# Linformer attention and SwiGLU on one core: E and F loaded as one stacked tile ahead of k, and the first units' turns in another order

## The chip, the core and the metric

The program runs on one core of a Trainium2 chip. A core has a matrix engine (TensorE, PE in the profile; its weight loads are shown as PEld), a vector engine (VectorE, DVE), an activation engine (ScalarE, ACT), a general engine (GpSimd, POOL) and a queue engine (SyncE, SP). Each runs its own list of instructions in order and waits for others on semaphores. Data comes and goes by DMA; a DMA is issued by SP, ACT or POOL, and all issued ones run on the core's 16 DMA engines. In the profile q1 is the DMA queue of SP, q10 that of ACT and q0 that of POOL. Matmul results go to PSUM, which the kernel divides into pools of banks; a bank is free again when its reader has copied it out.

The metric is the device time of one execution in microseconds, as the median of several runs. Beside it there is one profiled execution, from which all durations come.

## The reference

```python
k_proj = np.einsum('ks,bhsd->bhkd', E, k)        # E, F: 64 x 1024; q, k, v: 8 x 8 x 1024 x 64
v_proj = np.einsum('ks,bhsd->bhkd', F, v)
scores = (1 / sqrt(64)) * q @ k_proj^T            # 8 x 8 x 1024 x 64
attn = softmax(scores)
x = (attn @ v_proj), heads side by side           # 8192 x 512
g = x @ w_gate                                    # 512 x 1536
out = (g * sigmoid(g) * (x @ w_val)) @ w_out      # 8192 x 512
```

Every batch has its k and v projected over the sequence by E and F, from 1024 rows to 64; the attention is over these 64 rows. Its result goes through a gated feed-forward block. All inputs and the output are float32; the kernel multiplies in bfloat16.

## The kernel before

The feed-forward work is done in 16 chunks of 512 tokens (two for each batch), and each chunk in 12 tiles of 128 hidden columns: `f_g` makes the gate tile (four matmuls over x, then a tanh on ACT), `f_v` the value tile (four matmuls, then two VectorE operations that give hT), `f_y` the output. A loop over the 192 tiles (lines 629 to 637) runs these on TensorE, and `run_slot` puts the attention work of the next batches between them. That loop is the bulk of the time. The change does not touch it.

Before the loop stands a start written out by hand (lines 480 to 595), which brings the first chunk's x as early as it can. Its order is the order in the code: `manual_schedule` keeps it, for each engine and for each DMA queue. It does this:

- **Loads.** ACT's queue gets k of heads 0 and 1, k of heads 2 and 3 (two float32 pieces, `kraw`, 0.5 MB each) and then F. SP's queue gets E. POOL's queue casts while it loads and gets, in this order, a part of q, k of heads 4 to 7, the other part of q, v in three pieces, and the weights of hidden tiles 0 and 1 and of the next ones. Some of the weight loads stand in POOL's list behind the normalisations `u_N`.
- **Warming.** `warm(n)` runs n matmuls over zeros, whose results nobody reads.
- **Turning E and F.** The projection needs E and F with the sequence on the partitions. `turn(which, at, halves)` transposes 64x128 pieces on TensorE (lines 504 to 509) and copies four of them at a time to `ET` or `FT` on ACT (line 511, which shows as line 138, the helper `copy`). E is turned after eleven warming matmuls. F is turned in two halves, later, between other work.
- **Projecting k.** VectorE casts the four heads of `kraw` to bfloat16; ACT casts half of the last one (lines 531 to 536). `u_KV` multiplies with `ET` (line 150), first heads 0 to 3 and later 4 to 7; `u_KT0` turns the result and four copies put it into the block diagonal `BD`.
- **Units.** The first chunk has four units (u = 0 to 3: head group g = u // 2, token half i = u % 2). For each, `u_T` turns q, `u_S` makes the scores and their exponentials (lines 271 and 275), `u_R` sums them and takes the reciprocal on VectorE (lines 286 and 288), `u_N` multiplies (line 301, on POOL), and `u_A` turns the normalised unit (line 317) and copies it to `AT`.
- **Projecting v, and x.** `u_V0` multiplies v with `FT` (lines 170 to 185), `u_PV2` and `u_PV1` make x from `AT` and the projected v (lines 343 and 355), one or two head pairs and 256 tokens at a time.
- **The first tiles.** `f_mm(c, f, w, i)` (line 377) makes the half i (256 tokens) of hidden tile f; w is 0 for the gate and 1 for the value. Four such groups, for the first 256 tokens of tiles 0 and 1, stand among the last turns of the units (lines 576 to 582).

The PSUM pool "pa" (`ps_a`, letter "a") has three banks, used in turn by `u_T`, `u_A`, `u_PV2` and `u_PV1` and, before, by F's turn. Pools "g" and "v" have two banks each, pool "y" one.

Of the kernel before, what the change touches and what calls it, by code (L numbers as in the profile page):

```python
# [12 lines left out]
BF16 = mybir.dt.bfloat16  # L13
FP32 = mybir.dt.float32
# [3 lines left out]
S = 1024  # L18
D = 64
KP = 64  # L20
DM = H * D
DFF = 1536
P = 128
NJ = S // P
# [10 lines left out]
def kernel(  # L35
# [19 lines left out]
    nc = tc.nc  # L55
    scale = 1.0 / float(D) ** 0.5

    const = ctx.enter_context(tc.tile_pool(name="const", bufs=1))
# [15 lines left out]
    BD = [const.tile([P, H, P], BF16, name=f"BD{i}") for i in range(2)]  # L74
    BDV = [const.tile([P, NPAIR, P], BF16, name=f"BDV{i}") for i in range(2)]
    ks = [const.tile([P, H, D], BF16, name=f"ks{i}") for i in range(2)]
    ET = const.tile([P, NJ, KP], BF16, name="ET")
    FT = const.tile([P, NJ, KP], BF16, name="FT")

    wg = w_pool.tile([P, NKT, DFF], BF16, name="wg")  # L80
    wv = w_pool.tile([P, NKT, DFF], BF16, name="wv")
# [51 lines left out]
    def bank(where, shape, dt, name):  # L133
        pool, tag = banks[where]
        return pool.tile(shape, dt, name=name, tag=tag)

    def copy(eng, out, in_):
        (nc.scalar.copy if eng is nc.scalar else eng.tensor_copy)(out=out, in_=in_)  # L138
# [152 lines left out]
    def u_N(b, u, eng=nc.gpsimd):  # L291
        ch, w = divmod(u, 4)
        g, i = divmod(w, 2)
        if (b, ch) in BY_DMA:
            if (b, ch, "d") not in AA:
                AA[b, ch, "d"] = aw.tile([P, 4, H, KP], BF16, name="AAd", tag="AAd")
            a = AA[b, ch, "d"][:, 2 * i : 2 * i + 2, 4 * g : 4 * g + 4, :]
        else:
            a = AA[b, u] = aw.tile([P, 2, 4, KP], BF16, name="AA", tag="AA", bufs=4)
            a = a[:]  # L300
        eng.tensor_tensor(  # L301
            out=a.rearrange("p j h k -> p h j k"),
            in0=ee.pop((b, u))[:],
            in1=rr.pop((b, u))[:].unsqueeze(3).to_broadcast([P, 4, 2, KP]),
            op=ALU.mult,
        )
# [45 lines left out]
    def u_PV1(b, ch, pr, i, eng):  # L352

        ps = ps_a.tile([P, CW // 2], FP32, name="pv", tag="pa")
        nc.tensor.matmul(
            out=ps[:].rearrange("p (j t) -> p j t", t=P),
            lhsT=BDV[b % 2][:, pr, :],
            rhs=AT[b, ch][:, 2 * i : 2 * i + 2, pr, :],
            start=True,
            stop=True,  # L360
        )
        copy(eng, xT[b, ch][:, pr, 256 * i : 256 * (i + 1)], ps[:])
# [4 lines left out]
    half = {}  # L367
# [109 lines left out]

    with tc.manual_schedule():

        kb[0] = kv_pool.tile([P, H, NJ, D], BF16, name="kb", tag="kb")  # L480
        kraw = [aw.tile([P, 2, NJ * D], FP32, name="kraw", tag=tag) for tag in ("qTd", "AAd")]
        for i in range(2):
            nc.scalar.dma_start(
                out=kraw[i][:],
                in_=k[0, 2 * i : 2 * i + 2].rearrange("h (p j) d -> p h (j d)", j=NJ),
            )
        ef = []
        for which, src in (("E", E), ("F", F)):
            raw = const.tile([KP, S], FP32, name=f"{which}raw")
            (nc.sync if which == "E" else nc.scalar).dma_start(out=raw[:], in_=src)  # L490
            ef.append(raw)
        load_q(0, 0, (0, 2))
        load_k(0, 4, 8)
        zeros = const.tile([P, CW], BF16, name="zeros")
        nc.vector.memset(zeros[:], 0.0)
        make_identity(nc, ident_fp[:])
        make_identity(nc, ident_bf[:])
        nc.vector.memset(ks[0][64:P], 0.0)

        def turn(which, at, halves=(0, 1)):  # L500
            for half in halves:
                ps = bank(at, [P, 4, KP], FP32, "efp")
                for i in range(4):
                    j = 4 * half + i
                    nc.tensor.transpose(
                        out=ps[:, i, :],
                        in_=ef[which][:, bass.ds(j, P, step=NJ)],
                        identity=ident_fp[:KP, :KP],
                    )
                js = slice(4 * half, 4 * half + 4)  # L510
                copy(nc.scalar, (ET, FT)[which][:, js, :], ps[:])

        def warm(n):

            ps = bank("v", [P, CW], FP32, "warm")
            for _ in range(n):
                nc.tensor.matmul(
                    out=ps[:], lhsT=zeros[:, 0:P], rhs=zeros[:],
                    start=True, stop=True,
                )  # L520


        dve, act = nc.vector, nc.scalar
        load_q(0, 0, (2, 4))
        load_v(0, (0, 4, 6, 8))
        load_w_gv(0, 1)
        load_w_gv(1, 2, (0,))
        warm(11)
        turn(0, "v")
        warm(4)  # L530
        for h in range(4):
            for n in range(2):
                eng = act if (h, n) == (3, 1) else dve
                ds = slice(256 * n, 256 * (n + 1)) if h == 3 else slice(0, 512)
                if n == 0 or h == 3:
                    copy(eng, kb[0][:, h].rearrange("p j d -> p (j d)")[:, ds], kraw[h // 2][:, h % 2, ds])
        nc.vector.memset(BD[0][:], 0.0)
        u_KV(0, "k", (0, 4), at="y")
        warm(1)
        u_T(0, 0, "a", act)  # L540
        u_KT0((0, 2), "vg", (dve, dve, dve, act))
        turn(1, "a", (0,))
        u_T(0, 2, "a", act)
        u_S(0, 0, "g")
        u_R(0, 0)
        u_N(0, 0)
        load_w_gv(1, 2, (1,))
        load_w_gv(2, 4, (0,))
        turn(1, "a", (1,))
        warm(1)  # L550
        u_KV(0, "k", (4, 8), at="y")
        warm(1)
        u_KT0((2, 4), "vg", (dve, dve, act, act))
        u_T(0, 1, "a", dve)
        u_T(0, 3, "a", dve)
        u_S(0, 2, "g")
        u_A(0, 0, dve)
        u_R(0, 2)
        u_N(0, 2)
        u_S(0, 1, "g")  # L560
        u_R(0, 1)
        u_N(0, 1)
        u_S(0, 3, "v")
        u_R(0, 3)
        u_N(0, 3)
        u_V0(0, 2, "y")
        u_PV2(0, 0, 0, 0, act)
        warm(1)
        u_V0(2, 3, "y")
        u_A(0, 2, act)  # L570
        u_V0(3, 4, "v")
        u_PV1(0, 0, 2, 0, dve)
        u_PV1(0, 0, 3, 0, act)
        u_A(0, 1, dve)
        load_w_gv(2, 4, (1,))
        f_mm(0, 0, 0, 0)
        u_A(0, 3, act)
        u_PV2(0, 0, 0, 1, dve)
        f_mm(0, 0, 1, 0)
        f_mm(0, 1, 0, 0)  # L580
        u_PV2(0, 0, 1, 1, act)
        f_mm(0, 1, 1, 0)
        nc.vector.memset(ks[1][64:P], 0.0)
        nc.vector.memset(BD[1][:], 0.0)
        nc.vector.memset(BDV[1][:], 0.0)
        load_w_gv(4, 6)
        load_q(0, 1, hs=(0, 4))
        load_w_gv(6, 8)
        load_q(0, 1, hs=(4, 8))
        load_w_gv(8, 10)  # L590
        load_w_gv(10, 12)
        load_q(1, 0)
        load_k(1)
        load_wo(0)
        load_wo(1)

        for i, u in enumerate(range(4, 8)):
            put(11 + i, u_T, 0, u)
            put(13 + i, u_S, 0, u)
            put(14 + i, u_R, 0, u)  # L600
            put(14 + i, u_N, 0, u)
            put((17, 18, 20, 21)[i], u_A, 0, u, nc.scalar)
        put(19, u_PV, 0, 1, 0)
        put(20, u_PV, 0, 1, 1)
        put(22, u_PV, 0, 1, 2)
        put(22, u_PV, 0, 1, 3, nc.vector)
        put(20, load_v, 1)
        put(20, load_q, 1, 1)
        for b in range(1, B):
            place(b)  # L610
        for b in range(2, B):
            s0 = 48 * (b - 1) - (20 if b == 3 else 24)
            at = (43, 43, 44, 45) if b == 2 else (s0, s0 + 2, s0 + 4, s0 + 6)
            put(at[0], load_k, b)
            put(at[1], load_v, b)
            put(at[2], load_q, b, 0)
            put(at[3], load_q, b, 1)

        for s in slots:
            slots[s].sort(key=lambda x: x[0] not in (load_k, load_v, load_q))  # L620


        ypart = defaultdict(list)
        for c in range(B * CH - 1):
            for n in range(NFT):
                f = n if c else 4 + (2 * n + 1) // 3
                ypart[(c + 1) * NFT + f].append((c, n))

        for t in range(NIT):
            c, f = divmod(t, NFT)  # L630
            i = 1 if t < 2 else None
            f_g(c, f, i)
            run_slot(2 * t)
            f_v(c, f, i)
            for a in ypart.pop(t, ()):
                f_y(*a)
            run_slot(2 * t + 1)
        for n in range(9):
            f_y(B * CH - 1, n)
        f_y_last(B * CH - 1, 3)  # L640
        assert not slots and not ypart
# [29 lines left out]
```

The softmax here doesn't subtract the row's maximum and nothing guards it: scores larger than these inputs give would overflow.

## Time and profile before

| what | value |
|---|---|
| median of 10 runs | 568.91 us (568.68 to 569.68) |
| profiled execution | 568.9 us, of which its span is 567.1 us |
| TensorE busy | 560.5 us, 99% of the span |
| VectorE, ACT, POOL busy | 339.1, 235.7, 110.8 us |
| DMA | 62.91 MB, 111 GB/s on average |
| TensorE busy in the first 24.8 us | 21.69 us |

How to read it: busy times add up the durations of an engine's instructions. Matmuls overlap by their tails, so a group of four that is shown with 1.03 us takes its place for 0.86 us on the engine. TensorE is busy nearly all the time, but in the first 24.8 us part of the busy time is warming. In timelines a row has the start, the length, the engine, the line, the operation with its tiles and how many there are; in brackets stands how long the engine was idle before and what ended the idle time. In the chain of waits a row has its start, its length and what it was. From 24.8 us on the chain consists of TensorE's work, apart from a place at about 40 us with ACT in it.

### The profile page before, as it was taken

The page shows a single profiled execution, that of the slowest core. Times are in us where ns is not written, and L with a number is a line of the kernel's source. Part 1 is how long each engine was busy: PE and PEld are TensorE (multiplying, and loading weights), DVE is VectorE, ACT ScalarE, POOL GpSimd, SP SyncE. Part 2 cuts the span into 40 slices and gives each one's busy share as a digit, 9 for nine tenths or more (in the row PEclk, how much of TensorE's full clock was granted, in tenths as well). Part 3 has the DMA queues.
Part 4 walks back from the last instruction along what each step waited for, and adds up shares of the span by engine and source line. Part 5 has one row for each costly group of instructions (what it writes and reads, how often), then busy time and mean ns, then how long its engine had stood idle before and what let it go on. Part 6 is the DMA issues. An engine that isn't in the chain of part 4 may idle for free.

```text
span 567.1 us, 7942 instructions
## 1 busy us (share of the span) xinstructions
PE 560.5 (99%) x2970; PEld 266.5 (47%) x2970; DVE 339.1 (60%) x576; ACT 235.7 (42%) x416; POOL 110.8 (20%) x124
## 2 busy tenths in 40 slices
PE   8999999999999999999999999999999999999997
PEld 4654444444444444444444444444444444444444
DVE  3786664766476645765566655666547665545550
ACT  3564352444434443443435434354343543443322
POOL 6851250133012400133002230024100220000000
PEclk9999999999999999999999999999999999999999
DMA  9999999629913795029930499106990213101012
GB/s 210 178 198 188 174 149 201 132 57 190 197 41 74 118 202 108 38 57 165 183 80 37 77 187 201 38 19 112 194 178 19 62 39 68 38 37 38 19 38 93
DMA packets 111159, 62.91 MB, mean 111 GB/s; under 512 B 64272, under 2 KB 102416, under 8 KB 111120
## 3 DMA queue, kind: packets, MB, share of 16 engines
q0 software_dynamic: 42816, 29.36, 36.3%
q1 hardware_dynamic: 67392, 31.46, 26.2%
q10 hardware_dynamic: 912, 1.57, 0.9%
q8 instruction: 23, 0.38, 0.3%
q14 instruction: 16, 0.13, 0.1%
HBM read 60.29 MB, written 16.78 MB: 136 GB/s over the span
## 4 chain that ended last, share of the span: by engine, by line
PE 95%; DMA 4%; ACT 0%; issue 0%; DVE 0%; POOLq 0%
PE yps L415 29%; PE gps L377 29%; PE vps L377 29%; PE kvp L150 3%; PE sc L271 2%; PE pv L328 2%; DMA wg<-in_moe_w_gate_dram 2%; DMA qb<-in_q_dram 1%; ACT th L389 0%; PE qTp L237 0%; PE kTp L194 0%; DVE s L396 0%; PE aTp L317 0%; ACT AT L138 0%; ACT ysb L425 0%
## 5 line engine op out<-in xcount | busy, mean ns | idle before, releaser
L396 DVE SCALAR_TENSOR_TENSOR s<-th,gps 128x512 f32<-128x512 f32 x192 | 130.4, 679 | 134.5 <-ACT th L389 134.0
L377 PE MATMUL gps<-xT,wg 128*128 128x512 bf16 (+1 forms) x776 | 197.7, 377 | 0.4 <-DMA wg<-in_moe_w_gate_dram 0.3
L377 PE MATMUL vps<-xT,wv 128*128 128x512 bf16 (+1 forms) x776 | 197.5, 377 | 0.0
L415 PE MATMUL yps<-wo,hT 128*128 128x512 bf16 (+1 forms) x780 | 194.5, 376 | 0.0
L389 ACT ACTIVATE th<-gps 128x512 f32<-128x512 f32 x192 | 114.6, 597 | 159.1 <-PE gps L377 153.9
L401 DVE TENSOR_TENSOR hT<-s,vps 128x512 bf16<-128x512 f32 x192 | 132.0, 688 | 20.4 <-DVE s L396 0.5
L301 POOL TENSOR_TENSOR AAd<-ee,rr 128x512 bf16<-128x512 f32 x56 | 58.2, 1041 | 342.5 <-issue 184.8
L415 PEld LDWEIGHTS <-hT 128*128 128x128 bf16 x780 | 76.2, 98 | 89.9
L377 PEld LDWEIGHTS <-wv 128*128 128x128 bf16 x776 | 74.0, 98 | 83.3 <-issue 2.9
L377 PEld LDWEIGHTS <-wg 128*128 128x128 bf16 x776 | 73.9, 98 | 81.8 <-issue 1.2
L425 ACT ACTIVATE ysb<-yps 128x512 f32<-128x512 f32 (+1 forms) x65 | 38.4, 590 | 77.7 <-PE yps L415 77.7
L138 ACT CAST xT<-pv 128x512 bf16<-128x512 f32 (+1 forms) x62 | 35.9, 581 | 52.3 <-PE pv L328 50.3
L286 DVE TENSOR_REDUCE zz<-ee 128x8 f32<-128x512 f32 x64 | 43.5, 679 | 22.2 <-ACT ee L275 22.2
L275 ACT ACTIVATE ee<-sc 128x512 f32<-128x512 f32 x64 | 38.0, 596 | 19.4 <-PE sc L271 19.4
L271 PEld LDWEIGHTS <-qTd 128*128 128x128 bf16 x224 | 17.1, 98 | 13.4 <-DMA qTd<-qb 0.4
L328 PE MATMUL pv<-AT,BDV 128*128 128x512 bf16 x60 | 22.4, 379 | 0.1
L271 PE MATMUL sc<-BD,qTd 128*128 128x128 bf16 x224 | 21.7, 219 | 0.0
L288 DVE RECIPROCAL rr<-zz 128x8 f32<-128x8 f32 x64 | 13.0, 203 | 6.7 <-DVE zz L286 0.5
L108 POOL DMA_DIRECT2D qb<-in_q_dram x18 | 16.3, 908 | 1.4 <-POOLq L655 0.8
L150 PE MATMUL kvp<-kb,ET 128*64 128x512 bf16 (+1 forms) x72 | 15.5, 358 | 0.1
L162 DVE CAST BDV<-kvp 64x256 bf16<-64x256 f32 x7 | 3.0, 426 | 20.0 <-ACT ks L158 17.8
L150 PE MATMUL kvp<-vb,FT 128*64 128x512 bf16 x56 | 13.4, 382 | 0.0
(64 smaller groups left out, 137.4 us busy)
## 6 DMA issues: line engine op xcount, KB each, us to landing
out_dram<-ysb SPq DMA_DIRECT2D x63, 256.0 KB, 2.3
qb<-in_q_dram POOLq DMA_DIRECT2D x14, 512.0 KB, 18.0
kb<-in_k_dram POOLq DMA_DIRECT2D x7, 1024.0 KB, 11.0
vb<-in_v_dram POOLq DMA_DIRECT2D x7, 1024.0 KB, 14.7
wo<-in_moe_w_out_dram POOLq DMA_DIRECT2D x2, 768.0 KB, 22.7
wg<-in_moe_w_gate_dram POOLq DMA_DIRECT2D x5, 256.0 KB, 7.8
wv<-in_moe_w_val_dram POOLq DMA_DIRECT2D x5, 256.0 KB, 8.4
kraw<-in_k_dram ACTq DMA_DIRECT2D x2, 512.0 KB, 4.8
```

Source lines behind the costliest of these rows:

```text
L138: (nc.scalar.copy if eng is nc.scalar else eng.tensor_copy)(out=out, in_=in_)
L150: nc.tensor.matmul(out=t[lo : lo + 64, h0:h1].rearrange("p h d -> p (h d)"), lhsT=w[:, j, :], rhs=src[b][:, h0:h1, j, :], start=(j == 0), ...
L271: nc.tensor.matmul(out=ps[:, n, :], lhsT=t[:, n, :], rhs=BD[b % 2][:, 4 * g + n, :], start=True, stop=True)
L275: nc.scalar.activation(out=e[:].rearrange("p h j k -> p (h j k)"), in_=ps[:].rearrange("p a k -> p (a k)"), func=AF.Exp, scale=scale,)
L286: nc.vector.reduce_sum(out=z[:], in_=e[:], axis=AX.X)
L301: eng.tensor_tensor(out=a.rearrange("p j h k -> p h j k"), in0=ee.pop((b, u))[:], in1=rr.pop((b, u))[:].unsqueeze(3).to_broadcast([P, 4, 2 ...
L377: nc.tensor.matmul(out=ps[:, ts], lhsT=(wg, wv)[w][:, kt, f * P : (f + 1) * P], rhs=x[:, kt, ts], start=(kt == 0), stop=(kt == NKT - 1),)
L389: nc.scalar.activation(out=th[:], in_=ps[:], func=AF.Tanh, scale=0.5)
L396: nc.vector.scalar_tensor_tensor(out=s1[:], in0=th[:], scalar=1.0, in1=g[:], op0=ALU.add, op1=ALU.mult)
L401: nc.vector.tensor_tensor(out=hT[c][:, f, :], in0=s1[:], in1=ps[:], op=ALU.mult)
L415: nc.tensor.matmul(out=yy[c][:, cs], lhsT=hT[c][:, f, i * P : (i + 1) * P], rhs=wo[:, f, cs], start=(f == 0), stop=(f == NFT - 1),)
L425: nc.scalar.activation(out=ysb[:, cs], in_=yy[c][:, cs], func=AF.Copy, scale=0.5)
```

## The change

E and F go into one tile of 128 partitions, E in the lower half and F in the upper. E is loaded by SP's queue and F by ACT's; both issues now stand ahead of the k pieces. `turn_ef` transposes 128x128 pieces, which gives E and F side by side in one tile `EF`; it does so in two halves of four, one in a "g" bank and one in a "v" bank, each copied by ACT in one operation. F's two later turns go away. Eight warming matmuls stand before it and seven after it (there were eleven and four). VectorE casts all four heads of k. A warming matmul before `u_T(0, 0)` goes away, the one after F's second half becomes three, and the one after the first `u_PV2` goes away. Unit 3 is normalised by VectorE. The turn of unit 1 moves ahead of the second `u_PV1`, and the turn of unit 3 ahead of the weight load and the first `f_mm`.

```diff
-    ET = const.tile([P, NJ, KP], BF16, name="ET")
-    FT = const.tile([P, NJ, KP], BF16, name="FT")
+    EF = const.tile([P, NJ, 2 * KP], BF16, name="EF")
+    ET, FT = EF[:, :, 0:KP], EF[:, :, KP : 2 * KP]
...
+        efraw = const.tile([P, S], FP32, name="efraw")
+        nc.sync.dma_start(out=efraw[0:64], in_=E)
+        nc.scalar.dma_start(out=efraw[64:P], in_=F)
         kb[0] = kv_pool.tile([P, H, NJ, D], BF16, name="kb", tag="kb")
...
-        ef = []
-        for which, src in (("E", E), ("F", F)):
-            raw = const.tile([KP, S], FP32, name=f"{which}raw")
-            (nc.sync if which == "E" else nc.scalar).dma_start(out=raw[:], in_=src)
-            ef.append(raw)
...
-        def turn(which, at, halves=(0, 1)):
-            for half in halves:
-                ps = bank(at, [P, 4, KP], FP32, "efp")
+        def turn_ef():
+
+            for half in range(2):
+                ps = bank("gv"[half], [P, 4, 2 * KP], FP32, "efp")
                 for i in range(4):
-                    j = 4 * half + i
                     nc.tensor.transpose(
                         out=ps[:, i, :],
-                        in_=ef[which][:, bass.ds(j, P, step=NJ)],
-                        identity=ident_fp[:KP, :KP],
+                        in_=efraw[:, bass.ds(4 * half + i, P, step=NJ)],
+                        identity=ident_fp[:],
                     )
-                js = slice(4 * half, 4 * half + 4)
-                copy(nc.scalar, (ET, FT)[which][:, js, :], ps[:])
+                nc.scalar.copy(out=EF[:, 4 * half : 4 * half + 4, :], in_=ps[:])
...
-        warm(11)
-        turn(0, "v")
-        warm(4)
+        warm(8)
+        turn_ef()
+        warm(7)
         for h in range(4):
-            for n in range(2):
-                eng = act if (h, n) == (3, 1) else dve
-                ds = slice(256 * n, 256 * (n + 1)) if h == 3 else slice(0, 512)
-                if n == 0 or h == 3:
-                    copy(eng, kb[0][:, h].rearrange("p j d -> p (j d)")[:, ds], kraw[h // 2][:, h % 2, ds])
+            copy(dve, kb[0][:, h].rearrange("p j d -> p (j d)"), kraw[h // 2][:, h % 2])
         nc.vector.memset(BD[0][:], 0.0)
         u_KV(0, "k", (0, 4), at="y")
-        warm(1)
         u_T(0, 0, "a", act)
         u_KT0((0, 2), "vg", (dve, dve, dve, act))
-        turn(1, "a", (0,))
         u_T(0, 2, "a", act)
...
-        turn(1, "a", (1,))
-        warm(1)
+        warm(3)
         u_KV(0, "k", (4, 8), at="y")
...
-        u_N(0, 3)
+        u_N(0, 3, dve)
         u_V0(0, 2, "y")
         u_PV2(0, 0, 0, 0, act)
-        warm(1)
         u_V0(2, 3, "y")
         u_A(0, 2, act)
         u_V0(3, 4, "v")
         u_PV1(0, 0, 2, 0, dve)
+        u_A(0, 1, dve)
         u_PV1(0, 0, 3, 0, act)
-        u_A(0, 1, dve)
+        u_A(0, 3, act)
         load_w_gv(2, 4, (1,))
         f_mm(0, 0, 0, 0)
-        u_A(0, 3, act)
         u_PV2(0, 0, 0, 1, dve)
```

## The prediction

> **What bounds the kernel now.** I read the page first: TensorE's busy time and the chain that ended last.
>
> ```profile
> PE 560.5 (99%) x2970; PEld 266.5 (47%) x2970; DVE 339.1 (60%) x576; ACT 235.7 (42%) x416; POOL 110.8 (20%) x124
> PE 95%; DMA 4%; ACT 0%; issue 0%; DVE 0%; POOLq 0%
> ```
>
> TensorE is the bound, and 4% of the chain is DMA. The chain in order of time says where (start, length, what):
>
> ```profile
> 1.25 8.14 DMA qb<-in_q_dram
> 9.39 0.28 issue
> 9.68 11.79 DMA wg<-in_moe_w_gate_dram
> 21.46 0.05 issue
> 21.51 0.61 PE gps L377 x4
> 22.12 0.22 PE pv L343 x2
> ...
> 23.43 0.61 ACT th L389
> 24.03 0.02 issue
> 24.05 0.70 DVE s L396
> 24.75 0.04 issue
> 24.80 1.02 PE gps L377 x4
> ```
>
> All the DMA stands before 21.5 us; from 24.80 on TensorE follows itself, and the change touches nothing later. So I ask one thing: when does the matmul group that began at 21.51 (hidden tile 1, gate, first 256 columns; call it G1) begin now? From G1 to 24.80 everything hangs on it (G1, pv, ACT's xT copy, tanh, VectorE's s, which frees the bank). What G1 moves, the end moves.
>
> G1 waits for two things. One is its weights, landed at 21.46. The other is TensorE's own program, read from the timeline by engine (start, length, engine, what, idle before):
>
> ```profile
> 1.19 4.40 PE L517 MATMUL warm<-zeros 128*128 128x512 bf16 x11 [1.19 <-DVE zeros L495]
> 2.88 0.15 PEld L517 LDWEIGHTS <-zeros 128*128 128x128 bf16 x1 [0.28 <-issue]
> 3.30 0.15 PEld L517 LDWEIGHTS <-zeros 128*128 128x128 bf16 x1 [0.28 <-issue]
> 5.93 1.07 PE L505 MATMUL efp<-ident_fp,Eraw 64*128 64x64 f32 x8 [0.34 <-DMA Eraw<-in_E_dram]
> 7.14 0.99 DVE L138 CAST kb<-kraw 128x512 bf16<-128x512 f32 x2 [1.58 <-DMA kraw<-in_k_dram]
> 8.18 1.03 PE L150 MATMUL kvp<-kb,ET 128*64 128x256 bf16 x8
> 12.35 1.06 PE L150 MATMUL kvp<-kb,ET 128*64 128x256 bf16 x8
> 20.64 0.60 PE L377 MATMUL vps<-xT,wv 128*128 128x256 bf16 x4
> ```
>
> The last row is the group before G1: four matmuls 0.11 apart, so TensorE was free for G1 at about 21.1 and waited 0.4 for the weights. The k projection of heads 0 to 3 began at 8.18, when VectorE had cast the second k piece, which landed at 7.14. That landing is what the change puts at risk.
>
> **The start, with E and F first.** F's issue (0.53 us on ACT's queue) goes ahead of both k issues, which move from 0.74 and 1.25 to about 1.27 and 1.75. E keeps its place as the first issue of SP's queue. POOL's queue issues its loads in the same order. The three queue tables below (packets, MB, share) are of 2.3 to 3.5, of 4.5 to 6 and of 6.5 to 7.5 us; q10 is ACT's queue, q1 SP's, q0 POOL's:
>
> ```profile
> q10 hardware_dynamic: 227, 0.46, 100.0%
> ...
> q10 hardware_dynamic: 212, 0.43, 100.4%
> ...
> q10 hardware_dynamic: 66, 0.24, 80.3%
> q0 software_dynamic: 170, 0.04, 45.1%
> ```
>
> Alone, ACT's queue moves 0.46 MB in 1.2 us, 387 GB/s. In the third table F (the third transfer of that queue) shares the engines with q loaded by POOL and moves 0.24 MB in 1.0 us, 240 GB/s. Now the second k piece is that third transfer. E, F and the first k piece are 1.05 MB: at 387 GB/s from 2.3 they end at 5.0. The second piece (0.52 MB) ends at 6.35 unshared, 7.2 shared as F was. From the last bytes to the landing it was some 0.9 us for that piece and 1.6 for F (7.5 to its landing at 9.07). The landing is thus 7.2 at best, 8.1 to 8.8 if shared. I take 8.4, shared, because F's row is nearest: same queue, same place, same rival load. VectorE then casts two whole heads (1.05 us for a pair) where ACT took half of one (0.99 in all), so the projection moves from 8.18 by d = 8.4 - 7.14 + 0.06 = 1.3 us; the ends for d are 0.1 and 1.7.
>
> Is TensorE ready by then? Eight warming matmuls at 0.43 end at 4.6. E and F (0.52 MB at 387 from 2.3, plus 0.9) land at about 4.6. A transpose of 64 columns took (1.07 - 0.27)/7 = 0.11 us; with 128 columns it takes between 0.11 and double that. I take double, 0.22, as matmuls here cost by columns (0.11 for 256, 0.215 for 512). Eight end by 6.4, seven more warming ones at 0.215 by 7.95. ACT's two copies of 128x512 (0.58 each, the xT row) replace two of 0.37 and are done by 7.2. So this part is hidden behind the k landing in every case but the third rival. It removes F's two turns later on.
>
> [...]
>
> **From there to the second projection.** Between them ran F's two half turns (0.65 each) and warming matmuls. Now the scores of unit 0 (last matmul at 11.33) are followed by three warming matmuls, 0.65, and the projection: 11.38 + 0.65 + 0.1 = 12.13 + d against 12.35. That saves 0.22, say 0.25 with F's copies gone from ACT. The k of heads 4 to 7 (landed 11.7) does not hold it at d = 1.3.
>
> **The units' turns.** One warming matmul (0.215) goes at 17.37, but the turn of unit 2 then waits for POOL's normalisation (17.9), so 0.13 is left. Unit 3's normalisation leaves POOL (1.04) for VectorE. The nearest row is VectorE's 128x512 f32 to bf16 product, 0.69; the ends are 0.41 (its copy of that size) and 1.04. It lies in VectorE's idle 1.17 us before 19.48, so it costs nothing. Were that cover gone, the pv copy queued behind it would wait, and the turn of unit 3 behind that. POOL's next weight issues come 1.04 earlier than 19.88, for weights first used at 25.66: no gain on the path. Unit 3's data is ready at 19.0 instead of 19.93. Yet its turn, now ahead of hidden tile 0, takes the third "pa" bank, free only when VectorE has copied pv: 19.35 + 0.42, so about 19.85. The first gate group slips from 19.69 to 20.06, and TensorE is free for G1 at 21.16 instead of 21.10. The new order gains nothing: between -0.2 and +0.2, and I take +0.06.
>
> **The sum.** G1 can start at 21.16 - 0.25 + d = 20.9 + d, and not before its weights. Those come through POOL's queue behind the same 1.57 MB of E, F and k, so they land at 21.46, or up to 0.4 earlier if the slow spell of 4.5 to 6 us (0.43 MB in 1.5 us, 290 GB/s) does not recur. With d = 1.3 G1 starts at 22.2 against 21.51: +0.7 us. The profiled execution took 568.9 (span 567.1 and 1.8 around it), the median 568.91: predicted 569.6. A measurement tells 0.2% (1.1 us) from nothing, so this counts as no change.
>
> **Rivals.**
> 1. *k is not hindered* (d = 0.1 to 0.4): k was served ahead of q in the old run (no q0 row between 4.5 and 6). Against it: the second piece now stands one place further back. G1 then waits for its weights, at 21.1 to 21.5, so 568.5 to 568.9. More can't be had: TensorE is not free before 20.9.
> 2. *Both k pieces fall behind q* (slower). The place is ACT's queue at 3.7 us. If q is ready then, the first piece shares too: 1.05 MB at 240 GB/s is 4.4 us from 3.7, 8.1, plus 0.9 to 1.6: landing 9.0 to 9.7, d = 1.9 to 2.6, +1.3 to +2.0, 570.2 to 570.9. It decides from a landing of 8.85 on. Against it: q had been issued at 1.25 and was not served at 3.6, when E was.
> 3. *TensorE stays slow.* The warming rows stand 0.43 apart until about 5.0 and 0.215 after. Eight instead of eleven lead up to that point, then come transposes. If the slow rate lasted through them, they would take 3.4 us from 4.7, the seven others 3.0: projection at 11.1, d = 2.9, +2.3 us, 571.2. If it ended at 8.1, d = 1.5: +0.9. For the fast end: the busy stretch is unbroken from 1.19 but for a wait of a few tenths. [...]
> 4. *The change does not do what it says*: as worked out, the VectorE normalisation and the new places bring nothing to G1. This is in the sum already.
>
> **How the numbers follow.** Forecast case (shared k, d 1.0 to 1.7, 569.3 to 570.0, or a little over with other slips): 0.50, of which 0.10 is beyond 570.05. Rival 1: 0.27, of which 0.03 is faster than 567.8 through something I do not see. Rival 2: 0.13. Rival 3: 0.10, half of it beyond the bound. Slower: 0.10 + 0.13 + 0.05 = 0.28, and I add 0.04 for small slips that sum up: 0.32. Faster 0.03, same 0.65. The range runs from rival 1's lower end, 568.5, to rival 2's, 570.8; what is left out is rival 3's end and the faster part.
>
> **What would show it.** In the changed profile: the second k cast of VectorE ending its wait at about 8.4 (rival 1: 7.2; rival 2: 9 or later); the first projection at 9.5; efp rows of 0.22 after 4.7 (0.43 in rival 3); the second projection at 13.4; unit 3's turn waiting for VectorE; G1 at 22.2 behind TensorE's own work, not behind a DMA, and the back-to-back stretch from 25.5. I am wrong if G1 still waits for its weights, or if idle time of TensorE appears after 26 us.

## The result and the profile after

The changed kernel took 573.35 us (median of 9 runs, 570.94 to 574.70) against 568.92 (31 runs, 568.68 to 570.54) for the kernel before: a ratio of 1.0071, with an interval of 1.0062 to 1.0081. It is slower, by 0.7% (4.0 us by the ratio, 4.4 between the medians), and outside the predicted range of 568.5 to 570.8. The profiled execution took 572.35, of which its span is 570.6.

The page of the changed kernel, busy times and the chain's shares by engine:

```profile
PE 560.0 (98%) x2962; PEld 266.1 (47%) x2962; DVE 339.9 (60%) x577; ACT 235.1 (41%) x413; POOL 109.8 (19%) x123
PE 96%; DMA 1%; DVE 1%; ACT 0%; ACTq 0%; issue 0%
```

TensorE does as much as before (560.0 us against 560.5) in a span that is 3.5 us longer. DMA's share of the chain fell from 4% to 1%, since the chain no longer runs through the long wait for weights. The chain in order of time, up to where TensorE follows itself:

```profile
1.36 0.86 ACTq L486
2.22 0.03 issue
2.25 8.13 DMA kraw<-in_k_dram
10.38 0.02 issue
10.41 0.96 DVE kb L138 x2
11.37 0.04 issue
11.41 1.86 PE kvp L150 x8
...
16.28 1.01 PE kvp L150 x8
...
22.20 1.13 DVE AA L301
23.34 0.35 DVE xT L138
...
25.20 0.44 PE gps L377 x4
...
27.57 0.70 DVE s L396
28.27 0.04 issue
28.31 1.02 PE gps L377 x4
```

The back-to-back stretch starts at 28.31 instead of 24.80, and from there to the end of the span it is 542.3 us in both profiles. So all 3.5 us were lost before it, and the one DMA in this part of the chain is the second k piece: landed at 10.38, where it had been 7.14. The timeline by engine shows what TensorE did meanwhile (in brackets idle time before, and what ended it):

```profile
1.20 3.57 PE L514 MATMUL warm<-zeros 128*128 128x512 bf16 x8 [1.20 <-DVE zeros L493]
5.58 1.13 PE L503 MATMUL efp<-ident_fp,efraw 128*128 128x128 f32 x8 [0.82 <-DMA efraw<-in_F_dram]
6.55 1.67 PE L514 MATMUL warm<-zeros 128*128 128x512 bf16 x7
7.20 0.96 DVE L138 CAST kb<-kraw 128x512 bf16<-128x512 f32 x2 [5.68 <-DMA kraw<-in_k_dram]
11.41 1.86 PE L150 MATMUL kvp<-kb,EF 128*64 128x256 bf16 x8 [3.19 <-DVE kb L138]
16.21 1.06 PE L150 MATMUL kvp<-kb,EF 128*64 128x256 bf16 x8
25.04 0.60 PE L377 MATMUL gps<-xT,wg 128*128 128x256 bf16 x4
```

The turn of E and F and the fifteen warming matmuls around it are over by 8.2. Then TensorE stands idle for 3.19 us, until VectorE has cast the late k piece, and the projection that follows takes 1.86 us instead of 1.03. The stretches of time say why (from:to, length, busy time of PE, PEld, DVE, ACT and POOL, the granted TensorE clock, DMA share, GB/s):

```profile
5.00:8.20 3.20, 2.62 (x15) 1.62 (x16) 0.96 (x2) 1.07 (x2) 3.20 (x5) 1.00 1.30 295
8.20:11.40 3.20, 0.02 (x1) 0.06 (x1) 0.94 (x2) 0.00 (x0) 1.22 (x2) 1.00 1.28 220
11.40:14.90 3.50, 3.14 (x20) 2.17 (x20) 1.29 (x4) 0.95 (x2) 0.00 (x0) 0.51 1.48 197
```

After the idle stretch the granted clock is 0.51. By the trace's clock events it was half from 11.44 to 14.85, 3.41 us, and full again after that. In the profile before it stays full from 4.98 us to the end.

What slowed the k piece is in the queue tables of 6 to 8 and of 8 to 10.4 us (packets, MB, share of the 16 engines' time; q0 is POOL's queue with q, q10 is ACT's with k):

```profile
q0 software_dynamic: 701, 0.18, 89.9%
q10 hardware_dynamic: 182, 0.36, 52.3%
...
q0 software_dynamic: 595, 0.37, 105.5%
q10 hardware_dynamic: 110, 0.19, 24.4%
```

In these stretches both queues are served together. k gets 0.36 MB in 2 us (180 GB/s) and then 0.19 MB in 2.4 us (80 GB/s), against 387 GB/s alone in the profile before.

The executions differ more than those of the kernel before. The ones with a granted clock of 1.000 and 0.999 took 570.94 and 571.76 us, those at 0.997 took 572.35 and 572.80, those at 0.994 took 572.65 to 574.23, and the one at 0.991 took 574.70. Half rate over 3.41 us takes 0.003 off the mean clock of the span (half of 3.41 in 570.6), so the median execution (0.994) fits two such stretches where the profiled one (0.997) had one.

### The profile page after: what moved, and what is told of

Same layout as the page of the kernel before. It is cut to its first block, busy times and chain, and to the rows that moved or that the text cites. A ratio compares the mean times of both kernels' runs of the same rounds, so it can differ in the third digit from the quotient of the medians.

```text
span 570.6 us, 7919 instructions
## 1 busy us (share of the span) xinstructions
PE 560.0 (98%) x2962; PEld 266.1 (47%) x2962; DVE 339.9 (60%) x577; ACT 235.1 (41%) x413; POOL 109.8 (19%) x123
## 4 chain that ended last, share of the span: by engine, by line
PE 96%; DMA 1%; DVE 1%; ACT 0%; ACTq 0%; issue 0%
PE yps L415 29%; PE gps L377 29%; PE vps L377 29%; PE kvp L150 3%; PE sc L271 2%; PE pv L328 2%; DMA kraw<-in_k_dram 1%; DVE zz L286 0%; DVE BD L138 0%; PE qTp L237 0%; ACT th L389 0%; DVE AA L301 0%; PE aTp L317 0%; DVE kb L138 0%; ACTq L486 0%
## 5 line engine op out<-in xcount | busy, mean ns | idle before, releaser
L150 PE MATMUL kvp<-kb,EF 128*64 128x512 bf16 (+1 forms) x72 | 16.3, 373 | 3.2 <-DVE kb L138 3.2
L150 PEld LDWEIGHTS <-EF 128*64 128x64 bf16 x128 | 8.6, 112 | 12.6 <-issue 7.4
```

The source lines that it names most:

```text
L150: nc.tensor.matmul(out=t[lo : lo + 64, h0:h1].rearrange("p h d -> p (h d)"), lhsT=w[:, j, :], rhs=src[b][:, h0:h1, j, :], start=(j == 0), ...
```

## The experiments

Two theories stood against each other from the start. *Order*: E and F ahead of k make the k piece late, q's load makes it later, and the idle TensorE loses its clock. *Rest*: the wider turn, the fewer warming matmuls, VectorE's normalisation or the new order of turns cost something by themselves. Each ratio below is to runs of the kernel before on the same chip and in the same group of runs.

### The order of the loads alone

The kernel before, with the block that loads E and F moved ahead of the k issues, and nothing else:

```diff
+        ef = []
+        for which, src in (("E", E), ("F", F)):
+            raw = const.tile([KP, S], FP32, name=f"{which}raw")
+            (nc.sync if which == "E" else nc.scalar).dma_start(out=raw[:], in_=src)
+            ef.append(raw)
         kb[0] = kv_pool.tile([P, H, NJ, D], BF16, name="kb", tag="kb")
...
-        ef = []
-        for which, src in (("E", E), ("F", F)):
-            raw = const.tile([KP, S], FP32, name=f"{which}raw")
-            (nc.sync if which == "E" else nc.scalar).dma_start(out=raw[:], in_=src)
-            ef.append(raw)
```

> The kernel before with one edit: the issues of E (SP's queue) and F (ACT's queue) stand ahead of the two k pieces; E and F are still turned apart, as before. Theory 1 (the second k piece, now third in ACT's queue, lands late, and TensorE's idle wait for it then costs it its full clock): second k piece lands at 9.5 us or later instead of 7.14, first projection at 10.5 or later, granted clock below 1.0 in most runs, median 571 to 574. Rival A (the stacked turn of 128 columns and its larger copies delay the projection) and rival B (the units' part: VectorE's normalisation and the new turns): neither is in this kernel, so 568.6 to 569.2.

Measured: 573.72 us (4 runs, 572.26 to 574.34), ratio 1.0070 (1.0046 to 1.0093). Its timeline:

```profile
10.15 0.63 DVE L138 CAST kb<-kraw 128x512 bf16<-128x512 f32 x2 [1.24 <-DMA kraw<-in_k_dram]
10.83 1.87 PE L150 MATMUL kvp<-kb,ET 128*64 128x256 bf16 x8 [2.70 <-DVE kb L138]
16.64 1.92 PE L150 MATMUL kvp<-kb,ET 128*64 128x256 bf16 x8
```

The order of the loads alone brings as large a loss as the full change: a late landing (10.13, against 10.38 in the changed kernel), the same half-rate projection, the same ratio. This is what the first theory expected. The make-up of its profile (span 572.5 us) is not quite the same: the clock stayed at half three times as long, from 9.6 to 19.8, so that the second projection ran slowly too, and TensorE later waited 0.6 us for value weights. Two of the three stretches (columns as above):

```profile
9.60:13.00 3.40, 2.17 (x9) 1.32 (x9) 1.11 (x3) 0.67 (x2) 0.74 (x1) 0.50 1.46 196
13.00:16.40 3.40, 3.40 (x26) 2.59 (x24) 0.86 (x3) 2.31 (x7) 0.00 (x0) 0.50 1.27 206
```

So equal ratios do not prove that the rest of the change is worth exactly nothing; the next runs bear on that.

### The units' part alone

The kernel before, with VectorE's normalisation of unit 3, the new places of the two turns and without the warming matmul that stood there:

```diff
-        u_N(0, 3)
+        u_N(0, 3, dve)
         u_V0(0, 2, "y")
         u_PV2(0, 0, 0, 0, act)
-        warm(1)
...
         u_PV1(0, 0, 2, 0, dve)
+        u_A(0, 1, dve)
         u_PV1(0, 0, 3, 0, act)
-        u_A(0, 1, dve)
+        u_A(0, 3, act)
         load_w_gv(2, 4, (1,))
         f_mm(0, 0, 0, 0)
-        u_A(0, 3, act)
```

> The kernel before with the units' part alone: unit 3 normalised by VectorE, the turns of units 1 and 3 at their new places, the warming matmul after the first pv group gone. Theory 1: this part is worth nothing, 568.7 to 569.2, G1 between 21.3 and 21.7 us. Rival B: part of the 4.4 us is here, 569.5 or more; the row to look at is the VectorE product, 1.13 us in the changed kernel against the 0.69 that was assumed.

Measured: 568.97 us (10 runs), ratio 0.9987 (0.9975 to 1.0000). The gate group of hidden tile 1 starts at 21.38 instead of 21.51. A further run takes the kernel before with only VectorE's normalisation:

```diff
-        u_N(0, 3)
+        u_N(0, 3, dve)
```

> The kernel before with unit 3 normalised by VectorE and nothing else. If the freed POOL is worth something to the kernel before: 568.5 to 568.8 and closer runs; if that product's 1.13 us delays the turn of unit 3 as much as it gives: 568.8 to 569.2.

Measured: 568.88 us (11 runs), ratio 0.9996 (0.9987 to 1.0005). So of *Rest* the units' part neither costs nor, measurably, saves. The wider turn and the fewer warming matmuls at the start were not run by themselves; in the changed profile both are over by 8.2 us, before k has landed.

### Warming until k is there

The changed kernel, with enough warming matmuls to leave no gap:

```diff
         turn_ef()
-        warm(7)
+        warm(20)
```

> The changed kernel with twenty warming matmuls after the turn of E and F instead of seven, so that TensorE has work until about 10.9 us and idles for half a microsecond at most before the projection at 11.4. If the idle wait of 3.2 us is what halves the clock: granted clock 1.0 in every run, first projection 1.0 us long instead of 1.86, median 570.6 to 571.3 and runs close together, since the one execution of the changed kernel with clock 1.0 took 570.94. If the clock falls for another reason (fewer warming matmuls at the start, the transposes): median near 573.3 and as wide a spread as before.

Measured: 572.84 us (7 runs, 571.20 to 573.42), ratio 1.0053 (1.0037 to 1.0069). In the timeline of its profiled execution (571.48 us) k is as late as before, and the projection is fast again:

```profile
6.84 4.48 PE L514 MATMUL warm<-zeros 128*128 128x512 bf16 x20
10.31 1.07 DVE L138 CAST kb<-kraw 128x512 bf16<-128x512 f32 x2 [2.16 <-DMA kraw<-in_k_dram]
11.43 1.03 PE L150 MATMUL kvp<-kb,EF 128*64 128x256 bf16 x8
```

So the half clock is the price of the gap, 0.83 us in a profile (1.86 against 1.03). The granted clock was 0.999 or 1.000 in all seven runs. But the median missed the expected 570.6 to 571.3, and by the ratios only 1 of the 4 us is back. The runs fall into two groups, 571.20 to 571.65 and 572.84 to 573.42, and the granted clock does not separate them. Two more executions of the same kernel, with no edit, were meant to catch the upper group:

> The third experiment again, for a trace of one of its slower executions (572.8 to 573.4 beside 571.2 to 571.7, both at full clock). If the k landing differs from run to run: an execution near 573 shows the second k cast at 11.5 to 12 instead of 10.3. If a later load is late (as in the first and the seventh experiment, where TensorE waited for value weights behind POOL's late issues): the cast at 10.3 and a wait of TensorE for weights between 34 and 40 us. An execution near 571.4 shows neither.

> As the run before it: one more execution of the same kernel, with the same two readings.

Measured: 571.38 and 570.80 us, neither in the upper group. What makes that group stays open. The two do show that k's landing itself varies, and the time with it: the last two casts start at 10.47 in the first and at 9.73 in the second, and the projection at 11.32 and 10.72.

### The second k piece on SP's queue

The changed kernel, with the second k piece issued by SP, behind E:

```diff
-            nc.scalar.dma_start(
+            (nc.scalar, nc.sync)[i].dma_start(
                 out=kraw[i][:],
```

> The changed kernel with the second k piece issued by SP, behind E, instead of by ACT behind F and the first piece. If the place in ACT's queue is what makes it late: it lands at 7.0 to 8.0 us, first projection at 8.2 to 9.1, TensorE never idle for 3 us, clock 1.0, median 568.8 to 569.8. If all transfers only share one pot of bandwidth with q, and the place does not matter: both k pieces land between 8.5 and 10, projection at 9.6 to 11, median 570 to 573.

Measured: 570.00 us (10 runs, 569.97 to 570.34), ratio 1.0010 (1.0001 to 1.0020). Its queue table of 4 to 6 us and its timeline:

```profile
q1 hardware_dynamic: 269, 0.52, 85.8%
q10 hardware_dynamic: 60, 0.10, 15.4%
```

```profile
8.26 1.64 DVE L138 CAST kb<-kraw 128x512 bf16<-128x512 f32 x4 [6.74 <-DMA kraw<-in_k_dram]
9.95 1.03 PE L150 MATMUL kvp<-kb,EF 128*64 128x256 bf16 x8 [1.89 <-DVE kb L138]
```

The second piece now moves 0.52 MB between 4 and 6 us, before q takes hold, and lands at 6.7; it is the first piece, behind F on ACT's queue, that comes last (8.2), and VectorE casts all four heads after it, in 1.64 us. The gap shrinks to 1.89 us, the granted clock is 1.0, and some 3 of the 4 us are back. So the place in the queue decides when the second piece lands, but the projection (9.95) and the median miss what that case expected, 8.2 to 9.1 and at most 569.8, since nothing was said there of the first piece. These ten runs also agree within 0.4 us.

### q behind the first transfers

The kernel with 20 warming matmuls, with POOL's first two loads issued after the two identities that POOL builds:

```diff
-        load_q(0, 0, (0, 2))
-        load_k(0, 4, 8)
         zeros = const.tile([P, CW], BF16, name="zeros")
...
         make_identity(nc, ident_bf[:])
+        load_q(0, 0, (0, 2))
+        load_k(0, 4, 8)
```

> The kernel of the third experiment (changed kernel, twenty warming matmuls) with POOL's first two loads (q, and k of heads 4 to 7) issued after the two identities instead of before them, about 1.3 us later. If q's packets running beside the second k piece are what makes it late and makes runs differ: it lands at 8.3 to 9.3 instead of 10.3, median 569.9 to 571.0, runs within 0.6 of each other. If the lateness is only the two transfers that now stand ahead of it: 10.0 to 10.4 as before, median 571.2 to 572.9 with the same two groups of runs; the later q could then cost another 0.5.

Measured: 571.80 us (7 runs, 570.91 to 573.46), ratio 1.0046 (1.0031 to 1.0061). The queue table of 6 to 8 us and the timeline:

```profile
q10 hardware_dynamic: 270, 0.51, 72.4%
q0 software_dynamic: 411, 0.11, 52.1%
```

```profile
6.49 4.48 PE L514 MATMUL warm<-zeros 128*128 128x512 bf16 x20
8.98 0.76 DVE L138 CAST kb<-kraw 128x512 bf16<-128x512 f32 x2 [1.04 <-DMA kraw<-in_k_dram]
10.90 1.06 PE L150 MATMUL kvp<-kb,EF 128*64 128x256 bf16 x8
```

With q later, k moves 0.51 MB in the 2 us where it had moved 0.41 in the run with 20 warming matmuls, and lands at 8.96 instead of 10.3, as expected if q's packets are what delays it. POOL's issue of q came only 0.51 us later (1.76 instead of 1.25), and not the 1.3 that the expectation took. The median misses the range of that case: the 20 warming matmuls now end after the cast, so the earlier landing is not used. With 13 of them instead:

```diff
-        warm(20)
+        warm(13)
```

> The fifth experiment with thirteen warming matmuls instead of twenty. In the fifth the k piece had landed at 8.96 and was cast by 9.74, but the twenty warming matmuls, ahead of the projection in TensorE's list, ended at 10.97 only. With thirteen (end at 9.5) the projection begins at 9.8 to 10.0 if k's landing decides, G1 at about 22.9, median 570.0 to 570.8. If the later q load decides (q now lands about 1 us later and is needed right after the projection): no better than the 571.0 of that profile.

Measured: 570.28 us (10 runs, 569.89 to 571.54), ratio 1.0022 (1.0012 to 1.0032). Its timeline:

```profile
8.99 0.76 DVE L138 CAST kb<-kraw 128x512 bf16<-128x512 f32 x2 [1.23 <-DMA kraw<-in_k_dram]
9.80 1.03 PE L150 MATMUL kvp<-kb,EF 128*64 128x256 bf16 x8 [0.30 <-DVE kb L138]
```

With q issued later the piece landed at 8.96 in both, with q at its old place at 9.7 to 10.5 in the three profiles of the kernel with 20 warming matmuls. This shift of q is thus worth 0.8 to 1.5 us of landing, 1.3 between the runs that were compared first. The other 1.8 us (8.96 against 7.14) are not split: they hold the place behind E and F, and what is left of q's load, as 411 of its packets still ran beside the piece from 6 to 8 us.

### k first, E and F stacked

The changed kernel, with F's issue back behind both k pieces:

```diff
-        nc.scalar.dma_start(out=efraw[64:P], in_=F)
...
+        nc.scalar.dma_start(out=efraw[64:P], in_=F)
         load_q(0, 0, (0, 2))
```

> The changed kernel with F's issue put back behind the two k pieces, as in the kernel before; E and F are still stacked and turned together. Theory 1: k lands at 4.5 and 7.1 again, but now the turn has to wait for F, which lands at about 9.1: turn from 9.1 to 10.2, copies done at 10.9, first projection at 10.9 to 11.1 with TensorE idle from 4.8 to 9.1, so the clock is lost too: median 571.5 to 574. So the stack itself forces either k or F to be late. If only the order of issue is at fault: median 568.7 to 569.5.

Measured: 574.06 us (4 runs), ratio 1.0082 (1.0064 to 1.0100). Its timeline:

```profile
7.53 1.05 DVE L138 CAST kb<-kraw 128x512 bf16<-128x512 f32 x2 [1.98 <-DMA kraw<-in_k_dram]
9.68 1.95 PE L503 MATMUL efp<-ident_fp,efraw 128*128 128x128 f32 x8 [4.89 <-DMA efraw<-in_F_dram]
11.41 2.54 PE L514 MATMUL warm<-zeros 128*128 128x512 bf16 x7
13.89 1.06 PE L150 MATMUL kvp<-kb,EF 128*64 128x256 bf16 x8
```

Now F is the one that lands late, at 9.54, and the stacked turn has to wait for it. The loss is larger than the landing alone: the projection begins at 13.89, where 10.9 to 11.1 was expected. The turn took 1.95 us and the seven warming matmuls behind it 2.54, against 1.13 and 1.67 in the changed kernel, since TensorE was at half rate up to about 13.1: the weight loads of the warming matmuls stand 0.43 us apart from 11.84 to 13.12, and the projection behind them took 1.06, as at full rate. The granted clock of this execution reads 1.0 all the same, as it does in the profile before from 1.2 to 4.5 us, where the warming matmuls stand 0.43 apart too. So a granted clock of 1.0 does not exclude that in the upper group of the kernel with 20 warming matmuls TensorE came to full rate later, for instance because eight warming matmuls open the kernel and not eleven; no trace of that group was kept.

With q's load at its old place, what stood third on ACT's queue landed at 9 to 10.4 in three profiles: F at 9.07 in the kernel before, k at 10.38 in the changed one, F at 9.54 here. The kernel before puts there what it needs last: it turns F in two halves after the first projection, the first of them at 9.89. The stack makes F as urgent as E.

### Weights in the order of use

Not a part of the change, but the place where the kernel before still waited: its weight loads and first groups in the order gate 0, gate 1, value 0, value 1, first alone and then with VectorE's normalisation of unit 3.

```diff
-        load_w_gv(0, 1)
+        load_w_gv(0, 1, (0,))
         load_w_gv(1, 2, (0,))
+        load_w_gv(0, 1, (1,))
...
-        f_mm(0, 0, 1, 0)
         f_mm(0, 1, 0, 0)
         u_PV2(0, 0, 1, 1, act)
+        f_mm(0, 0, 1, 0)
         f_mm(0, 1, 1, 0)
```

> Not a part of the change: the kernel before with the weights of the first two gate tiles loaded ahead of the first value tile's, and the matmuls of the first 256 tokens in the order gate 0, gate 1, value 0, value 1. If what holds the kernel before is its 0.4 us wait for the weights of gate tile 1 and the chain from there (x copy, tanh, s): gate 1 begins at 20.7 instead of 21.5, the back-to-back stretch at 24.2 instead of 24.8, median 0.4 to 0.6 us below the kernel before. If the lagging load only moves to value 0: within 0.2 us of it.

> The seventh experiment with unit 3 normalised by VectorE, as the change has it, and the turns at their old places. If the seventh lost its 0.5 us to later weights, which POOL issues only after its normalisations: POOL is free 1 us earlier, no wait for the value weights at 33.5, median 568.2 to 568.7, below both kernels. If VectorE's 1.13 us in the chain costs as much as it gives: 568.8 to 569.2.

Measured: 569.18 us (12 runs), ratio 0.9995 (0.9987 to 1.0003), and 568.63 us (11 runs), ratio 0.9995 (0.9986 to 1.0004). In the profiles the gate group of tile 1 starts at 21.09 and (in the chain) at 20.71 instead of 21.51, and the back-to-back stretch at 24.80, as before, and at 24.51. So the first misses its hoped-for 0.4 to 0.6 us: value weights are late next (the waits of the first of the two, in all, times and longest):

```profile
PEld L377 <- DMA wv<-in_moe_w_val_dram: 0.5, 1, 0.5
```

Neither can be told from the kernel before. No version here beat it clearly.

## Why the prediction was wrong

**What held.** The question asked was the right one: the end moves with the start of the gate group of hidden tile 1. The rule for it, 20.9 us plus the delay d of the first projection against 8.18, is tested by eight profiles of kernels with the stacked turn and the new order of the units:

| kernel | first projection | 20.9 + d | measured start of the group |
|---|---|---|---|
| changed | 11.41 | 24.13, and 0.83 for the half clock: 24.96 | 25.04 |
| 20 warming matmuls | 11.43 | 24.15 | 24.18 |
| the same, second and third profile | 11.32, 10.72 | 24.04, 23.44 | 24.05, 23.49 |
| k on two queues | 9.95 | 22.67 | 22.70 |
| q later, 20 and 13 matmuls | 10.90, 9.80 | 23.62, 22.52 | 23.67, 22.54 |
| k first, stacked | 13.89 | 26.61 | 26.65 |

The rule is good to 0.1 us. So the two steps in it, 0.25 saved before the second projection and 0.06 for the new order of turns, stand in their sum, and the run of the units' part bears out that it brings nothing that can be measured. The turn of E and F is hidden in the changed kernel, the group no longer waits for weights, and no idle time appeared after 26 us that the kernel before did not have (542.3 us in both). So neither of the two signs of being wrong that the prediction named came; what came was its mark of rival 2, a second cast at 9 us or later (10.41).

**What failed: the size of the landing.** The step was "I take 8.4, shared, because F's row is nearest". It measured 10.38. Two things made it up, by an estimate from the queue tables one microsecond each: the first three transfers ended at about 6 and not at 5.0, and the second piece landed 4.4 us behind them and not 3.4.
- E, F and the first k piece were to end at 5.0, at the 387 GB/s of k alone, and E and F to land at 4.6. In the changed profile all queues together moved 246 GB/s from 2 to 4 us and 271 from 4 to 6, so the three ended at about 6. F landed at about 5.4 and the first k piece at 7.2. ACT's first k issue also took 0.86 us where the prediction had half a microsecond.
- The second piece was to move at 240 GB/s, as F did. It moved at 180 and then 80. F's row differs in two ways. It was of one microsecond in which POOL's queue had 170 packets, while the piece met 701 in 2 us. And F's packets were larger: 66 for 0.24 MB, 3.6 KB each, against 182 for 0.36 MB, 2.0 KB each, for k. Per microsecond k's queue was served 91 packets from 6 to 8 us, more than F's 66, and still moved fewer bytes. No run separates the two; that more of q's packets leave fewer to k is seen across the runs (from 6 to 8 us 411 of q beside 270 of k with q later, 571 beside 209 with 20 warming matmuls, 701 beside 182 here). The row was the nearest by place, but neither by load nor by packets.

In the profile before there was a row with k and q served at once, from 6 to 6.5 us, when 0.98 of k's 1.05 MB had moved and the end of the second k piece met q:

```profile
q0 software_dynamic: 220, 0.06, 112.6%
q10 hardware_dynamic: 48, 0.07, 39.8%
```

That is 140 GB/s, and not 240.

With d = 3.23 in place of 1.3 this term is 1.9 us too small. Rival 2 came nearer with its price (landing 9.0 to 9.7), but not for its reason: it had both k pieces behind q. In the changed profile the first piece moved nearly alone from 4 to 6 us, and only the second met q:

```profile
q10 hardware_dynamic: 275, 0.53, 96.9%
q0 software_dynamic: 39, 0.01, 4.9%
```

**What was missing: the clock after a gap.** The prediction let TensorE finish its warming at 7.95 and start the projection at 9.5, a gap of 1.5 us, and put no price on a longer one. Rival 3 priced a half clock, but at the transposes, where it did not occur (eight in 1.13 us, full clock from 4.61). It came at the projection, for 0.83 us. A late landing and a lost clock were two cases in the list, while here the first brought about the second.

The sum in the profiled execution: 0.7 predicted, 1.93 for the landing, 0.83 for the clock, 0.07 left over, together the 3.5 measured. The median lies 1.0 us above that execution; its clock of 0.994 fits a second half-rate stretch, which no profile of the changed kernel shows.

**Smaller sizes.** A transpose of 128 columns took (1.13 - 0.27)/7 = 0.12 us, like one of 64 and not double. VectorE's product took 1.13 us, above the upper end of 1.04 taken from POOL; the row of 0.69 was a product of another form. Neither moved the end by more than the rule's 0.1 us. The cover of the product was used up, though: the chain of the changed kernel runs through it (22.20, and the copy behind it at 23.34).

**The shared case.** From 6 to 10.4 us q0 and q10 were served in the same stretch (701 and 182 packets from 6 to 8, 595 and 110 from 8 to 10.4); in what order their packets went the tables do not show. So k and q did share, as the forecast case has it; its 569.6 was too small by the sizes above. E and F, two halves of one tile loaded on two queues, landed at 4.4 and 5.4 us, one after the other; whether one transfer for both would be quicker was not run.

## What to carry to other kernels

Before a transfer is moved ahead of another, list what each queue has in flight over the new landing, and price the displaced transfer by a row with that load and with packets of its size, not by the row of the transfer that stood in its place. If the landing feeds TensorE, add up the gap it makes: with gaps of 2.70 and 3.19 us the work behind ran at half rate for 3.4 us or more, with one of 1.89 us it did not. Joining two inputs in one operation makes both as urgent as the earlier one: in each order of these loads that was run with the stack, k or F came late. Others, such as F behind E on SP's queue and both k pieces first on ACT's, were not run.

## What the runs showed of the hardware

- How long the clock stayed at half was not the same in two profiles, and the length of the gap alone did not decide when it fell. In the changed kernel's profile it fell at 11.44, at the end of a gap of 3.19 us, and stayed at half for 3.41 us. In the run of the load order it fell at about 9.6, some 1.5 us into a gap of 2.70 us, and stayed three times as long, to about 19.8.
- In that run the first of the three stretches held 2.17 us of TensorE's work and no transposes, the middle one was busy throughout (3.40 us of 3.40), some 2.4 us of it with transposes, and the clock stayed at 0.50 after both. In the run with k first TensorE was at half rate up to about 13.1, some 3.4 us after it began at 9.68, and 1.95 us of these were float32 transposes. What made the half rate last longer in the run of the load order, and whether the transposes had a part in it, was not shown.
- A gap of 1.89 us in the profile with k on two queues cost no clock: the projection behind it took 1.03 us, at a granted clock of 1.0.
- The price of a half-rate stretch may not always be 0.83 us: nine executions of the kernel before, taken beside the experiments, had a granted clock of 0.996 or 0.997 and took 570.2 to 571.5 us, where the medians beside them were 569.0 to 569.4. No trace of one was kept, so what else differed in them is open.
- q's load took much of the engines' time for few bytes. Its packets were of some 250 bytes: 170 of them in a microsecond (0.04 MB) took 45% in the profile before, 701 in 2 us (0.18 MB) took 90% in the one after. The k transfer alone, in packets of 2.0 KB, took 100% for 0.46 MB in 1.2 us.
